# Two chunks of the second MLP's weights converted during the first routing, and the first expert's weight split placed after the token gathers

## The chip, the core and the metric

One NeuronCore of a Trainium2 chip runs the whole program. The metric is the device time of one execution in microseconds (us). The engines are TensorE (PE in the rows, its weight loads PEld), VectorE (DVE), ScalarE (ACT), GpSimd (POOL) and SyncE (SP, which here issues nearly all DMAs). Each engine works through its own instructions in the order in which the program lists them; semaphores make it wait for the others.

## The reference

Three layers follow each other, all in float32 at the interfaces: a decayed linear attention over 8 sequences of 576 tokens, a mixture of 8 experts in which every expert takes exactly 576 of the 4608 tokens by a greedy global order of the gate's logits, and a two-layer MLP with a squared ReLU.

```python
# attention (8 batches, 8 heads, 576 tokens, 64 wide); gamma by head
ret = scale * (q @ k.T) * Dmat          # Dmat = gamma ** (i - j) for i >= j
x = (ret @ v) -> (4608, 512)
# experts: tokens in descending order of logits, each expert takes 576
logits = x @ w_gate
for idx in argsort(-logits.flatten()):  # assign token to expert while it has room
    ...
out[mask_e] = relu(x[mask_e] @ w1[e]) @ w2[e]
# second MLP, 4608 tokens, 512 -> 2048 -> 512
h = relu(x @ w_in); return (h * h) @ w_out
```

`w_in` and `w_out` come as float64 (they are a float32 array times a NumPy scalar), so the kernel has to bring 64-bit numbers to 32 bits itself.

## The kernel before

**Stages.** The program has three stages. Attention (`attention`, up to about 175 us of the span) walks over 36 tiles of 128 tokens; tile t does the key transposes of tile t+2 (L145, L147), the scores of tile t+1 (L167, L171), the part of the state (L199), the values (L207, L210) and the state's update (L181, L187). The result x^T stays in nine SBUF buffers named `big`. The second stage is what is called here the routing gap (about 175 to 219 us): `Router.phase(0)` searches by counting for the 576 tokens of the first expert, on VectorE and TensorE in turns (L401 to L438), while `turn_back` transposes x^T back and writes the rows of x to memory (`xd`, L661 to L665). The third stage alternates `moe(k)` for expert k and one or two calls of `mlp(j)` for 384 tokens each; it takes the rest, with a matmul nearly always on TensorE. There the router's steps for later experts are strewn between the matmuls (`slot`).

**Precision.** Every float32 operand of a large matmul is split into a rounded high part and a low part, and three products are summed (`PAIRS`). So each chunk of weights is split before use: two copies on ScalarE (L631), one subtraction on GpSimd (L632), one on VectorE (L633). `pump()` does this for one chunk and issues the load of a later one; `pump(True)` issues the load alone.

**The second MLP's weights.** `convert` is a generator with 32 units (16 chunks in two halves). One call of `next(filler)` at the end of each attention tile moves all live units one step: load the raw 64-bit half (L559), two steps later three ScalarE operations (L564 to L566), one step later three VectorE operations (L570 to L572), two steps later the write of the 32-bit result to memory (`wd`, L575). Nine chunks (`RES`) are later read back and stay in SBUF: `stay` loads eight of them from `wd` during the first expert, `part` splits them (L690, L691), and the ninth goes through two buffers named `xg`.

**Between routing and the first expert.** The main loop (L892 to L896) takes one step of the router, one or two tiles of `turn_back`, and one `pump`, which splits only once the last one-hot comparison of list 0 is issued (`near`). When the list is there (L513 to L518), `load_tokens` gathers the tokens' rows by five indirect DMAs on GpSimd's queue (L711), `turn` transposes each gathered tile (L719) and splits it into XH (ScalarE, L727) and XL (VectorE, L728). Until three tiles are turned, nothing of the first expert starts; 36 transposes into a scratch tile (L900) keep TensorE busy while the gathers run. Then `moe(0)` begins with L805 (first layer), L810 and L811 (ReLU and its low part), L788 (second layer).

**What sets the order.** There is no scheduler: every engine's order is the order of the Python code. All tiles come from pools with a fixed number of buffers that are handed out in rotation, so a new tile of a name waits until the last reader of the tile some places back is done: `h` has 3 buffers, `ot` 3, `mm` (PSUM) 3, `raw` 3, `big` 9, `xg` 4, and `gs`, the gate's staging tile, 1.

## Time and profile before

| | us |
|---|---|
| median of 3 runs | 1510.81 |
| lowest and highest of them | 1508.19, 1512.13 |
| the profiled execution, as timed | 1512.18 |
| its span in the profile | 1510.4 |
| attention, to the router's first step | 0 to 175.4 |
| routing gap, to the first expert's first matmul | 175.4 to 219.3 |
| experts and second MLP | 219.3 to the end |

The profile is one execution taken by the hardware profiler. Its time lies 1.37 us above the median of the three runs, and 1.78 us of it lie outside the span. All times of instructions are counted from the span's start. A row of the timeline says when an engine did what, and in square brackets how long the engine had stood idle before it and what released it; a row of windows gives the busy time of each engine in a stretch. Matmuls overlap, so a "busy" TensorE says that it had work, not that it was at its peak.

### The profile page before, as it was taken

To read this page: it belongs to the slowest core of one execution; us is meant where nothing else is said; L and a number is where in the kernel's file an instruction comes from. 1 tells how busy PE (TensorE), PEld (TensorE's weight loads), DVE (VectorE), ACT (ScalarE), POOL (GpSimd) and SP (SyncE) were. 2 spreads that over 40 slices of the span, in tenths; PEclk is the share of its full clock that TensorE was granted. 3 is DMA by queue.
4 is the path that set the end of the run, shared out by engine and by line. 5 is a ranking of instruction groups with operands and counts; after the bars stand their busy time and mean duration, and the time that the engine had idled before them with its cause. 6 is when DMAs were issued, how large, how long until landed. Compare 5 with 4: busy or idle time off the path is not lost.

```text
span 1510.4 us, 27450 instructions
## 1 busy us (share of the span) xinstructions
PE 1461.7 (97%) x10599; PEld 1325.1 (88%) x10599; DVE 933.6 (62%) x1965; ACT 688.6 (46%) x1349; POOL 468.6 (31%) x410
## 2 busy tenths in 40 slices
PE   7998879999999999999999999999999999999997
PEld 6777768888988889989988899899888999999896
DVE  4989768767664667656665676566656544454341
ACT  6766544444533345335433354345334454454332
POOL 4555124444311334124213143143112441251110
PEclk9999989999999999999999999999999999999999
DMA  9999477224511326225312153245113352262200
GB/s 335 346 354 359 177 252 265 85 84 125 169 43 63 102 66 194 70 91 160 113 56 95 56 154 119 77 125 162 57 49 102 116 184 64 63 195 77 70 29 21
DMA packets 64354, 201.14 MB, mean 133 GB/s; under 512 B 8416, under 2 KB 8800, under 8 KB 64224
## 3 DMA queue, kind: packets, MB, share of 16 engines
q1 hardware_dynamic: 58272, 179.99, 36.3%
q0 software_dynamic: 5952, 19.40, 3.8%
q8 instruction: 83, 1.36, 0.4%
q14 instruction: 47, 0.39, 0.1%
HBM read 172.10 MB, written 27.26 MB: 132 GB/s over the span
## 4 chain that ended last, share of the span: by engine, by line
PE 84%; DVE 7%; issue 4%; ACT 3%; DMA 1%; POOL 0%; SPq 0%; POOLq 0%; DVEq 0%; ACTq 0%
PE mm L868 25%; PE acc L852 24%; PE acc L788 13%; PE mm L805 13%; PE px L207 2%; PE sc L167 1%; PE mm L719 1%; PE rps L511 1%; DVE cb L572 1%; DVE G L401 1%; DVE A L171 1%; DVE w L633 1%; PE px L199 1%; ACT cb L564 1%; PE pr L145 1%
## 5 line engine op out<-in xcount | busy, mean ns | idle before, releaser
L632 POOL TENSOR_TENSOR w<-raw,w 128x512 fp32r<-128x512 f32 x212 | 278.4, 1313 | 817.7 <-ACT w L631 783.1
L633 DVE TENSOR_TENSOR w<-raw,w 128x512 fp32r<-128x512 f32 x212 | 226.9, 1070 | 193.5 <-ACT w L631 192.5
L631 ACT ACTIVATE w<-raw 128x512 fp32r<-128x512 f32 x424 | 253.1, 623 | 78.3 <-PE acc L788 62.1
L852 PE MATMUL acc<-big,h 128*128 128x512 f32 x972 | 251.2, 399 | 1.8 <-ACT h L878 1.8
L788 PE MATMUL acc<-h,w 128*128 128x288 f32 x1536 | 223.4, 296 | 0.0
L852 PEld LDWEIGHTS acc<-big,h 128*128 128x128 f32 x972 | 180.8, 189 | 38.6 <-ACT h L878 2.9
L788 PEld LDWEIGHTS acc<-h,w 128*128 128x128 f32 x1536 | 208.5, 188 | 0.7 <-DVE h L811 0.4
L874 ACT ACTIVATE r<-mm 128x384 f32<-128x384 f32 x192 | 93.8, 488 | 237.7 <-PE mm L868 217.8
L878 ACT ACTIVATE h<-r 128x384 fp32r<-128x384 f32 x192 | 100.8, 525 | 216.7 <-DVE r L876 216.7
L852 PE MATMUL acc<-w,h 128*128 128x512 f32 x756 | 196.0, 398 | 2.9 <-DVE h L845 2.9
L876 DVE TENSOR_TENSOR r<-mm,r 128x384 f32<-128x384 f32 x192 | 106.0, 552 | 128.6 <-ACT r L874 127.9
L868 PE MATMUL mm<-YH,big 128*128 128x384 f32 x864 | 171.6, 340 | 0.0
L852 PEld LDWEIGHTS acc<-w,h 128*128 128x128 f32 x756 | 140.1, 189 | 29.9 <-DVE h L845 3.8
L805 PE MATMUL mm<-XH,w 128*128 128x288 f32 x1024 | 160.5, 299 | 0.8 <-ACT XH L727 0.7
L868 PEld LDWEIGHTS mm<-YH,big 128*128 128x128 f32 x864 | 151.2, 189 | 7.5 <-ACT YH L794 0.8
L845 DVE TENSOR_TENSOR h<-r,h 128x384 fp32r<-128x384 f32 x192 | 110.9, 578 | 65.6 <-ACT h L878 65.6
L805 PEld LDWEIGHTS mm<-XH,w 128*128 128x128 f32 x1024 | 143.2, 189 | 1.8 <-ACT XH L727 0.9
L868 PE MATMUL mm<-YH,w 128*128 128x384 f32 x672 | 134.0, 341 | 0.0
L868 PEld LDWEIGHTS mm<-YH,w 128*128 128x128 f32 x672 | 118.2, 189 | 4.3
L810 ACT ACTIVATE h<-mm 128x288 fp32r<-128x288 f32 x128 | 52.5, 410 | 103.2 <-PE mm L805 97.8
L868 PE MATMUL mm<-YL,big 128*128 128x384 f32 x432 | 92.8, 337 | 0.0
L805 PE MATMUL mm<-XL,w 128*128 128x288 f32 x512 | 89.1, 296 | 0.0
(171 smaller groups left out, 1749.8 us busy)
## 6 DMA issues: line engine op xcount, KB each, us to landing
raw<-we SPq DMA_DIRECT2D x128, 512.0 KB, 3.6
raw<-wd SPq DMA_DIRECT2D x84, 512.0 KB, 3.3
qk<-att SPq DMA_DIRECT2D x36, 512.0 KB, 6.7
craw<-wm SPq DMA_DIRECT2D x32, 512.0 KB, 6.7
v<-att SPq DMA_DIRECT2D x36, 256.0 KB, 5.4
wd<-cb SPq DMA_DIRECT2D x32, 256.0 KB, 5.6
xd<-YH SPq DMA_DIRECT2D x18, 256.0 KB, 3.7
xd<-YL SPq DMA_DIRECT2D x18, 256.0 KB, 3.7
```

The costliest lines, as they stand in the source:

```text
L631: nc.scalar.activation(w[:, 0], c, AF.Copy)
L632: nc.gpsimd.tensor_sub(w1[:, 1], raw[:, :512], w1[:, 0].bitcast(F32))
L633: nc.vector.tensor_sub(w2[:, 1], raw[:, 512:], w2[:, 0].bitcast(F32))
L788: nc.tensor.matmul(acc[part][d][:, :288], w2[:, wi, d * 128:(d + 1) * 128], h[:, xi, :288], start=(f == 0 and i == 0), stop=(f == 7 and i ...
L805: nc.tensor.matmul(p[:, :288], w1[:, wi, g * 128:(g + 1) * 128], X[xi][:, g, 288 * part:288 * part + 288], start=(g == 0 and i == 0), stop ...
L810: nc.scalar.activation(h[:, 0, :288], p[:, :288], AF.Relu)
L845: nc.vector.tensor_sub(h[:, 1], s, h[:, 0].bitcast(F32))
L852: nc.tensor.matmul(acc[t], h[:, xi, t * 128:(t + 1) * 128], w2[:, wi], start=(f == 0 and i == 0), stop=(f == 15 and i == 2))
L868: nc.tensor.matmul(p[:, :384], w1[:, wi, g * 128:(g + 1) * 128], Y[xi][:, g, o:o + 384], start=(g == 0 and i == 0), stop=(g == 3 and i == 2))
L874: nc.scalar.activation(r, p[:, :384], AF.Relu)
L876: nc.vector.tensor_mul(s, p[:, :384], r)
L878: nc.scalar.activation(h[:, 0], s, AF.Copy)
```

## The change

The change has five parts. (1) `convert` leaves out chunks 13 and 15 (`LATE`), so it has 28 units; one extra `next(filler)` ahead of the tile loop starts it one tile earlier. Conversions on ScalarE now stand behind tiles 1 to 28 instead of 2 to 33, on VectorE behind tiles 2 to 29 instead of 3 to 34. (2) `late_load` reads the raw 1 MB of each of the two chunks into a `big` buffer that x^T has left, after 12 and after 22 turned tiles; `late_units` converts them in place, with `ot` and `h` tiles as scratch: ScalarE's six operations of chunk 13 when `near` is set, VectorE's six behind the first four gathers, then ScalarE's six of chunk 15, and VectorE's six of chunk 15 behind the three turned tiles. (3) In the main loop nothing is split any more; the first split stands behind the first four gathers, the second behind the three turned tiles. So `moe(0)` begins with two chunks split instead of three. (4) The scratch transposes become 30, and 6 after each of the three turned tiles. (5) The last gates of the attention are issued inside the last tile, with two `gs` buffers; `stay` and `part` lose the two chunks, and `part` takes a step in every round of the second half of `moe(0)` instead of in every other one, the two late chunks first.

```diff
@@ gate, attention
-            gs = wk.tile([128, 512], F32, name="gs", bufs=1)
+            gs = wk.tile([128, 512], F32, name="gs", bufs=2)
...
         decay(1)
+        next(filler)
         for t in range(NT):
...
+            if t == NT - 1:
+                next(ready)
+                last = gate(32, 35)
+                next(last)
             values(t)
             if t % 9 != 8:
                 state(t)
             if t == NT - 2:
                 ready = rt.prep(0, 32)
-            if t >= NT - 2:
                 next(ready)
+            if t == NT - 1:
+                next(last)
...
-        last = [gate(32, 35), gate(35, 36, "sp")]
-        for g in last:
-            next(g)
-        for g in last:
-            next(g)
+        for _ in gate(35, 36, "sp"):
+            pass
@@ convert
+LATE = (13, 15)
+def scaled(nc, raw, b, n):
+    nc.scalar.activation(b, raw[:, :, 1].bitcast(F32), AF.Copy, scale=2.0 ** -112)
+    nc.scalar.activation(n, raw.bitcast(U16)[:, :, 1], AF.Copy, scale=2.0 ** -13, bias=2.0 ** 23)
+    nc.scalar.activation(n.bitcast(I32), n, AF.Copy, bias=-2.0 ** 23)
+def narrowed(nc, b, n, s, dst):
+    u = b.bitcast(I32)
+    nc.vector.tensor_scalar(s, u, -2147483648, None, op0=OP.bitwise_and)
+    nc.vector.scalar_tensor_tensor(s, u, 3, s, op0=OP.logical_shift_left, op1=OP.bitwise_or)
+    nc.vector.tensor_tensor(dst.bitcast(I32), s, n.bitcast(I32), op=OP.add)
...
-    todo = [(f, h) for f in range(16) for h in range(2)]
+    todo = [(f, h) for f in range(16) if f not in LATE for h in range(2)]
@@ body
+        def late_load(f):
+            late[f] = w = gp.tile([128, 2048], F32, name="big", bufs=9)
+            nc.sync.dma_start(w.bitcast(I32) if wide else w[:, :1024], a["wm"][f].bitcast(I32) if wide else a["wm"][f])
+        def late_units():
...
+            for f in LATE:
+                raw = late[f].bitcast(I32).rearrange("p (n t) -> p n t", t=2)
+                for h in range(2):
+                    if h:
+                        x = [wk.tile([128, 2, 384], R, name="h", bufs=3).bitcast(F32)
+                             .rearrange("p a b -> p (a b)")[:, :512] for _ in range(3)]
+                    else:
+                        x = [wk.tile([128, 512], F32, name="ot", bufs=3) for _ in range(3)]
+                    scaled(nc, raw[:, 512 * h:512 * h + 512], x[0], x[1])
+                    work.append((x, late[f][:, 512 * h:512 * h + 512]))
+                yield
+                for x, dst in work:
+                    narrowed(nc, x[0], x[1], x[2].bitcast(I32), dst)
+                work = []
+                yield
...
-            for n in ((0, 1), (2, 3), (4, 5), (6,), (7,)):
+            for n in ((0, 1), (2, 3), (4, 5)):
...
-                        if part and f % 2:
+                        if part:
                             next(parter, None)
...
-            pump(0 not in near)
+                turns += 1
+                if turns in (12, 22):
+                    late_load(LATE[turns == 22])
+            if 0 in near and 0 not in listed:
+                next(units, None)
+                near.clear()
+            pump(True)
...
-        warm = ps.tile([128, 512], F32, name="mm", bufs=3)
-        for _ in range(36):
-            nc.tensor.transpose(warm[:, :128], idn, idn)
+        for _ in range(4):
+            next(loader)
+        next(units, None)
+        pump()
+        next(units, None)
+        warm(30)
         while state["turned"] < 3:
+            n = state["turned"]
             next(loader)
+            if state["turned"] > n:
+                warm(6)
         pump()
+        next(units, None)
```

VectorE between the first turned tokens and the router's next step, before (XL is the tokens' low part, w a split weight chunk, m the first result of the router's preparation for list 1):

```order
L728 TENSOR_TENSOR XL<-mm,XH 128x4x128
L728 TENSOR_TENSOR XL<-mm,XH 128x4x64
L728 TENSOR_TENSOR XL<-mm,XH 128x4x128
L633 TENSOR_TENSOR w_3324<-raw,w_3324 128x512
L375 TENSOR_REDUCE m<-L 128x36
L376 TENSOR_TENSOR V<-L,m 128x288
```

And now, at the same place:

```order
L769 TENSOR_TENSOR XL<-mm,XH 128x4x128
L646 TENSOR_TENSOR w_3317<-raw,w_3317 128x512
L558 TENSOR_SCALAR ot<-ot 128x512
L559 SCALAR_TENSOR_TENSOR ot<-ot 128x512
L560 ISA big<-ot 128x1024
L558 TENSOR_SCALAR h<-h 128x512
L559 SCALAR_TENSOR_TENSOR h<-h 128x512
L560 ISA big<-h 128x1024
L378 TENSOR_REDUCE m<-L 128x36
```

The six operations that narrow chunk 15 stand ahead of the router's preparation; the six of chunk 13 stand in the same way ahead of the first weight split, behind the list's last operation.

ScalarE between the list's one-hot columns (HC) and the first tokens' high part (XH), before:

```order
L499 ACTIVATE HC<-h_113,rt 128x36x5
L631 ACTIVATE w_3217<-raw 128x512
L631 ACTIVATE w_3218<-raw 128x512
L631 ACTIVATE w_3247<-raw 128x512
L631 ACTIVATE w_3248<-raw 128x512
L727 ACTIVATE XH<-mm 128x4x128
```

And now, from the end of chunk 13's conversion on:

```order
L553 ACTIVATE h<-h 128x512
L644 ACTIVATE w_3221<-raw 128x512
L644 ACTIVATE w_3222<-raw 128x512
L551 ACTIVATE ot<-big 128x512
L552 ACTIVATE ot<-big 128x512
L553 ACTIVATE ot<-ot 128x512
L551 ACTIVATE h<-big 128x512
L552 ACTIVATE h<-big 128x512
L553 ACTIVATE h<-h 128x512
L768 ACTIVATE XH<-mm 128x4x128
```

Chunk 15's six operations stand between the first weight split and XH, and they write the `ot` and `h` tiles that VectorE reads for chunk 13.

GpSimd from the attention's last product on, before (xg are gathered rows):

```order
L154 TENSOR_TENSOR qh<-qk,qc 128x512
L632 TENSOR_TENSOR w_3217<-raw,w_3217 128x512
L632 TENSOR_TENSOR w_3247<-raw,w_3247 128x512
L711 DMA xg<-xd,idx 128x512
L711 DMA xg<-xd,idx 64x512
```

And now:

```order
L154 TENSOR_TENSOR qh<-qk,qc 128x512
L752 DMA xg<-xd,idx 128x512
L752 DMA xg<-xd,idx 64x512
L752 DMA xg<-xd,idx 128x512 x2
L645 TENSOR_TENSOR w_3221<-raw,w_3221 128x512
L752 DMA xg<-xd,idx 128x512
```

Four gathers come ahead of the first split and one behind it.

## Rows read from the trace of the kernel before

**Rows 1.** Page: busy time, share of the span and instructions of each engine.
```profile
PE 1461.7 (97%) x10599; PEld 1325.1 (88%) x10599; DVE 933.6 (62%) x1965; ACT 688.6 (46%) x1349; POOL 468.6 (31%) x410
```
**Rows 2.** Windows: start:end, length, busy us of each engine, granted clock, DMA share, GB/s.
```profile
150.00:155.00 5.00, 4.98 (x60) 4.27 (x62) 3.21 (x6) 0.97 (x3) 1.27 (x1) 0.66 0.68 224
...
200.00:220.00 20.00, 12.43 (x96) 11.03 (x94) 12.22 (x38) 5.75 (x11) 7.82 (x8) 0.74 0.74 243
...
400.00:500.00 100.00, 100.00 (x587) 90.77 (x586) 57.10 (x135) 39.24 (x78) 20.04 (x19) 1.00 0.23 77
```
**Rows 3.** Timeline, tile 3: start, length, engine, line, operation, [idle before <- releaser].
```profile
25.21 0.69 DVE L171 TENSOR_TENSOR A<-sc,mask 128x512 f32<-128x512 f32 x1 [1.24 <-PE sc L167]
```
**Rows 4.** Timeline, the attention's last tiles.
```profile
152.87 1.97 PE L207 MATMUL px<-A,v 128*64 128x128 f32 x16
...
158.82 1.09 PE L207 MATMUL px<-A,v 128*64 128x128 f32 x16
...
160.77 1.09 DVE L570 TENSOR_SCALAR cs<-cb 128x512 int32<-128x512 int32 x1
...
164.15 1.66 PE L167 MATMUL sc<-qk,kT 64*128 64x128 f32 x16
```
**Rows 5.** Timeline, one unit of the conversion on VectorE, and the router's first step.
```profile
170.12 0.42 DVE L570 TENSOR_SCALAR cs<-cb 128x512 int32<-128x512 int32 x1
...
171.39 0.69 DVE L572 CUSTOM_DVE_ANT_0 cb<-cs,cn 128x1024 uint16<-128x1024 uint16 x1
...
172.83 0.28 ACT L132 ACTIVATE gs<-sp 128x128 f32<-128x128 f32 x1 [0.70 <-PE pr L136]
...
175.41 0.95 DVE L401 SCALAR_TENSOR_TENSOR G<-kf,B,rt 128x448 f16<-128x448 f32 x2
```
**Rows 6.** Groups by line: the conversion's first ScalarE operation, count | busy, mean ns.
```profile
L564 ACT ACTIVATE cb<-craw 128x512 f32<-128x512 f32 x32 | 21.4, 668 | 0.0
```
**Rows 7.** Windows of 2 us in the routing gap, with the DMA share and rate last.
```profile
198.00:200.00 2.00, 0.34 (x5) 0.33 (x4) 1.71 (x4) 0.78 (x2) 0.00 (x0) 1.00 1.02 382
...
202.00:204.00 2.00, 0.01 (x1) 0.00 (x0) 1.79 (x10) 0.31 (x1) 0.00 (x0) 0.68 0.50 159
```
**Rows 8.** Timeline from the one-hot columns to the first expert's first matmul.
```profile
203.69 0.49 ACT L499 ACTIVATE HC<-h,rt 128x180 f16<-128x180 f16 x1 [2.67 <-DVE h L497]
...
207.80 1.35 DVE L633 TENSOR_TENSOR w<-raw,w 128x512 fp32r<-128x512 f32 x1 [0.96 <-DMA raw<-we]
...
209.26 1.03 DVE L517 TENSOR_TENSOR idx<-ids 128x4 int32<-128x4 f32 x1
...
210.58 1.13 POOL L711 DMA_INDIRECT xg<-xd,idx  x1 [0.30 <-DVE U L526]
...
217.50 0.85 PEld L719 LDWEIGHTS mm<-idn,xg 64*128 64x128 f32 x8 [2.80 <-DMA xg<-xd,idx]
...
219.27 1.89 PE L805 MATMUL mm<-XH,w 128*128 128x288 f32 x8 [0.69 <-ACT XH L727]
```
**Rows 9.** The line of the gathers, list 0 alone: from issue to landing.
```profile
DMA to landing us min/median/max: 3.5/3.8/4.6
```
**Rows 10.** Timeline, VectorE and TensorE in the first rounds of expert 0.
```profile
220.29 1.36 DVE L633 TENSOR_TENSOR w<-raw,w 128x512 fp32r<-128x512 f32 x1 [0.35 <-ACT w L631]
...
221.58 0.44 DVE L375 TENSOR_REDUCE m<-L 128x36 f32<-128x288 f32 x1
...
226.46 1.78 DVE L633 TENSOR_TENSOR w<-raw,w 128x512 fp32r<-128x512 f32 x1
...
228.30 1.81 DVE L401 SCALAR_TENSOR_TENSOR G<-kf,B,rt 128x448 f16<-128x448 f32 x2
...
229.91 0.49 PE L424 MATMUL rps<-A,G 128*128 128x64 f16 x5 [1.60 <-DVE G L401]
```
**Rows 11.** Timeline, two waits of TensorE in the first call of the second MLP.
```profile
300.50 1.91 PE L852 MATMUL acc<-w,h 128*128 128x512 f32 x7 [1.45 <-DVE h L845]
...
304.20 0.25 PE L483 MATMUL rps<-ones,DT 128*72 128x128 f16 x1 [1.79 <-DVE es L478]
```

32 lines of the change are left out of this document (19 added, 13 removed).

## The prediction

> **What bounds the kernel now.** I read the busy shares first: TensorE has work for 97% of the span [rows 1]. In the windows by stage it is full once the experts run (100 us of 100 between 400 and 500), and far from full in the routing gap, 12.43 us of 20 between 200 and 220 at a granted clock of 0.74 [rows 2]. So whatever this change brings or costs has to come out of the attention's end, the gap and the first rounds of expert 0; behind them it moves only if TensorE is made to wait. I then went through the timeline of those stretches in order of time and asked of every wait who ends it. In the attention TensorE sets the pace, and the conversion on ScalarE and VectorE only adds small stalls. In the gap the router's chain sets it, VectorE and TensorE in turns, up to the token list; then the gathers; then the turned tokens. In the first rounds of expert 0 it is VectorE: TensorE stands 1.60 us at L424 for VectorE's L401 [rows 10]. That last point matters most here.
>
> I count from the profiled execution, 1512.18 us; it lies 1.37 above the median of 1510.81, and the forecast goes to the median. A measurement of this kernel can tell about 0.3% from no change, 4.5 us, so "the same" is 1506.3 to 1515.3.
>
> **The attention.** One conversion unit on VectorE runs from 170.12 to 172.08, 1.96 us [rows 5]. Removed are four units of 32, and the conversion starts one tile earlier, so what is saved lies behind the last five tiles, and a unit is added behind tile 2. There VectorE has 1.24 us of idle [rows 3] for 1.96 of work: at most +0.7, at least 0, since rt.start's long casts that follow may swallow it; I take +0.4. At the end VectorE's L570 at 160.77 (1.09 us instead of 0.42) pushes the masks, and the scores at 164.15 take 1.66 us, held by it [rows 4, 5]; I put 0.5 of that down to the conversion and 0.2 to two short waits of TensorE for ScalarE. The regrouped gates drop the wait for the single `gs` buffer (0.70 at 172.83 [rows 5]), but their first four matmuls now stand ahead of the last tile's values; net -0.2. Together -0.9, between 0 and -2.5: the lower end is for the case that TensorE keeps its clock. Between 150 and 155 it was granted 0.66 [rows 2], and the same 16 matmuls took 1.97 us there against 1.09 later [rows 4]; over that tile about 1.6 us. The idle before that drop comes from a unit that stays (the last one, behind tile 29), so I don't count on it. The router's first step, at 175.41 [rows 5], comes 0.5 earlier.
>
> **The gap up to the list.** The two late loads are 2.1 MB, at the 382 GB/s of a full queue [rows 7] 5.5 us of DMA, and they stand in SP's queue ahead of the later writes of x. The queue is full up to 202 and half empty from there [rows 7], so the last write is through at about 207.5 instead of 202.5. The gathers read those rows, but can't start before the list does. So hidden, with about 1 us to spare; without that cover up to +2. ScalarE's copies wait for a write twelve tiles back; the second load delays this only for the last two tiles, which nobody awaits.
>
> **The list.** VectorE's first split starts at 207.80 and takes 1.35; the list's copy stands behind it, then an index operation takes 1.03 beside GpSimd's split, and the first gather is issued at 210.58 [rows 8]. With both splits behind the gathers the list is copied when its matmuls end, about 207.9, and the gather can go at 208.55: -2.0.
>
> **The turned tokens.** VectorE goes on with chunk 13: two units, 3.9 us, 209.5 to 213.4. ScalarE is done with HC at 204.18 [rows 8]; its six operations of chunk 13 at 0.67 each [rows 6] end at about 208.1. But chunk 15's six take the same scratch tiles and wait until VectorE has read them: the last ends at 214.85, and only then the first XH, which stood at 214.98 before. The gathers are no longer what is waited for: issued at 208.55, 209.85 and 211.1 and 3.8 us in flight [rows 9], the third is there at about 216. The scratch transposes rotate through the three `mm` buffers, so the third tile is turned behind the first XL; I get the third XH at 218.1 and L805 at 218.15 instead of 219.27 [rows 8]: -1.1 of the -2.0.
>
> A rule of the Trainium skill speaks against this part. The rows show gathers landing within 4.6 us while VectorE's index and split operations run [rows 9]. "SBUF — State Buffer", section "SBUF: two separate sides", says that VectorE's two-port operations lock GpSimd out of writing the descriptors of its own DMAs, so that such a DMA seems to be held up by VectorE; chunk 13's six operations now stand exactly beside the gathers. By the row the sum stays; by the page the gathers would be held, which is a rival below.
>
> **VectorE in expert 0.** The second weight split ended at 221.65 (220.29 and 1.36 [rows 10]); 1.0 earlier now. Behind it come chunk 15's two units, 3.9 us, and only then L375, at 224.55 instead of 221.58 [rows 10]: +3.0. What is queued behind: the router's preparation, the first low part L811, XL of the fourth tile, and L401, for which TensorE's L424 waits. From L375 to the end of L401 were 8.53 us, of which some 2.7 were VectorE operations held by GpSimd's splits (L633 1.78, L401 1.81, each about 1 us over its free length) and 0.65 were waits for XH. If none of this comes back, L401 ends at -0.4 against before; if all does, at +3.0. GpSimd still does the same three splits there, but one should meet reduces and PSUM reads, which ran at their free length beside it; and ScalarE is no longer late with XH. So I take off 1.0 and 0.65: +1.3. The -1.1 at L805 does not enter the sum, since L424 is later than all of it.
>
> **Behind that.** TensorE is full. GpSimd gets four more subtractions in expert 0's second half and four fewer in the first MLP call; the two waits there, 1.45 and 1.79 us [rows 11], could go or stay: I take 0, between -3.2 and +1. Two reads and four writes fewer on the queue release nobody.
>
> **Sum.** +0.4 - 0.9 + 1.3 = +0.8 against 1512.18; on the median 1510.81 + 0.8 = 1511.6.
>
> **Rivals.**
> *VectorE becomes the bound outright (slower).* One mechanism: chunk 15's six operations stand ahead of the router's preparation. If the third XH is as late as before and one GpSimd split holds one of the six (1.0), L375 comes at 226.5, +4.9, and if none of the 8.53 us is won back, TensorE stands over 5 us before L424 and comes back at a lower clock, as at 150 to 155; a 12-matmul group then loses 1.3. -0.5 + 4.9 + 1.3 = +5.7: 1516.5. It decides from L424 at about 234.5 on. For it: VectorE has almost no idle between 219 and 230. Against: TensorE's order gives it two groups to do in the meantime.
> *The stalls go (faster).* TensorE keeps its clock at 150 (-1.6), L401 comes at -0.4 instead of +1.3, and the two waits of rows 11 go (-3.2): +0.8 - 1.6 - 1.7 - 3.2 = -5.7: 1505.1. For it: all of these are small and sensitive to order. Against: the idle ahead of 150 has its cause in what stays.
> *The loads in x^T's places are not hidden.* The last write of x lands at 210.9 (207.2 and a landing of 3.7 us) and the gathers start 0.3 later than before instead of 2.0 earlier; everything behind comes as before plus chunk 15: +2.7, 1513.5. The change then doesn't bring the earlier gather that it makes room for.
> *The gathers are held by chunk 13.* If gathers 2 to 4 wait for the six operations to end at 213.4, the third lands at about 219, L805 stands at 220.6, and the sum grows by 2.4: 1514.0. The page named above would have it so; the rows so far don't.
>
> **How the numbers follow.** Forecast 0.50 (its own range 1508.6 to 1514.6), VectorE the bound 0.20, stalls go 0.13, loads not hidden 0.10, gathers held 0.07. Faster by over 0.3%: more than half of the second rival and the low tail, 0.11. Slower: most of the first, and some of the tails, 0.20. The same: 0.69. The range 1506.0 to 1517.0 leaves out the far ends of the first two rivals.
>
> **What would show it.** The first gather's issue should be near 208; the first XH right behind ScalarE's last operation of chunk 15; six VectorE operations ahead of the router's preparation; TensorE's wait at L424's successor longer than 1.60 and ending near 231; the router's first step near 174.9. Wrong would be: gathers landing after 217, a wait at the writes of x, a granted clock below 1 behind 232, or TensorE's waits at 300 and 304 gone.

## Result

The changed kernel takes 1520.97 us (median of six runs, 1519.79 to 1523.00) against 1510.99 for the kernel before (six runs on the same chip, 1508.19 to 1512.13): a ratio of 1.0068 with a 95% interval of 1.0057 to 1.0079. It is slower by 10 us. The forecast was 1511.6, 0.8 above the 1510.81 before, with a range to 1517.0; so the prediction said hardly any change, and the result lies 4 us outside its range. The profiled execution of the changed kernel has a span of 1519.3 us, that of the kernel before 1510.4.

The page's row of busy times, which answers to [rows 1]:

```profile
PE 1466.1 (96%) x10611; PEld 1327.9 (87%) x10611; DVE 934.1 (61%) x1965; ACT 687.6 (45%) x1349; POOL 468.6 (31%) x410
```

TensorE's busy time is 4.4 us longer, for the same matmuls and 12 scratch transposes more, some of them at the lower clock; the other half of the 9 us is waiting. Nearly all of both arises before the second expert begins. The next table is worked out from the timelines: the start of the router's first step on VectorE (`G`, L401 before, L404 after), of the first gather, of the first matmul of expert 0, of the first MLP call and of expert 1, and in the last two columns how long expert 0 and the first MLP call took. The later rows belong to the experiments below. From expert 1 on the distance between any of these kernels and the kernel before stays as it is, within 1 us, to the end, so the column of expert 1 decides.

| kernel | router | gather | expert 0 | MLP 0 | expert 1 | expert 0 takes | MLP 0 takes |
|---|---|---|---|---|---|---|---|
| before | 175.4 | 210.6 | 219.3 | 278.8 | 361.1 | 59.5 | 82.2 |
| after | 177.0 | 213.9 | 224.1 | 289.5 | 369.6 | 65.3 | 80.1 |
| b_loads | 174.1 | 215.1 | 225.0 | 284.7 | 367.1 | 59.7 | 82.3 |
| b_load1 | 174.1 | 212.0 | 221.6 | 281.6 | 362.5 | 60.0 | 80.9 |
| b_loads_late | 174.6 | 209.9 | 223.2 | 283.1 | 365.3 | 59.9 | 82.2 |
| b_split | 175.0 | 208.7 | 216.1 | 275.5 | 360.4 | 59.4 | 84.9 |
| b_split2 | 173.9 | 207.7 | 215.3 | 275.1 | 357.2 | 59.8 | 82.1 |
| b_split2p | 172.3 | 206.1 | 213.7 | 274.7 | 353.3 | 61.0 | 78.6 |
| u_split2 | 174.5 | 213.1 | 223.8 | 286.5 | 363.7 | 62.7 | 77.2 |
| u_skip15 | 174.5 | 213.1 | 222.9 | 283.7 | 363.6 | 60.8 | 79.9 |
| u_yh | 175.6 | 214.0 | 221.9 | 287.0 | 368.4 | 65.1 | 81.4 |
| u_13only | 175.0 | 210.1 | 219.2 | 281.1 | 361.0 | 61.9 | 79.9 |
| u_13split2 | 173.8 | 208.0 | 218.9 | 279.6 | 358.2 | 60.7 | 78.5 |

One caution belongs to it. The attention code of b_loads, b_load1, b_loads_late, b_split, b_split2 and b_split2p is that of the kernel before, and its end, the router's first step, lies between 172.3 and 175.4 from one profiled execution to the other. So a difference of one or two microseconds between two profiles is not an effect by itself; the timed ratios decide, and the columns show where. It helps to count from the router's first step: the gather comes 35.2 us behind it in the kernel before, 33.7 in b_split, 36.9 in the changed kernel, 38.6 in u_skip15 and 41.0 in b_loads.

**The gathers.** The forecast had the first gather at 208.55, 2.0 us sooner than before [rows 8]. It goes out at 213.87. The list is there at 209.7, as the row of VectorE's index operation (L520) shows, but the last six writes of x are only issued from 204.37 on and the fetch of weights behind them at 209.51, where the kernel before had reached it at 202.97. Even ScalarE, which copies x into the staging buffers, waits 3.51 us for an earlier write. Timeline of the changed kernel, from the second late load (L688) to the first matmul of expert 0:

```profile
195.44 1.26 SPq L688 DMA_DIRECT2D big<-wm  x1
...
204.37 4.93 SPq L678 DMA_DIRECT2D xd<-YL  x6
...
204.41 1.25 ACT L677 ACTIVATE YL<-mm 128x512 f32<-128x512 f32 x2 [3.51 <-DMA xd<-YL]
...
209.51 2.16 SPq L655 DMA_DIRECT2D raw<-we  x3
...
209.68 0.16 DVE L520 TENSOR_TENSOR idx<-ids 128x4 int32<-128x4 f32 x1
...
213.87 1.22 POOL L752 DMA_INDIRECT xg<-xd,idx  x1 [47.60 <-DMA raw<-we]
...
217.67 1.12 PE L760 MATMUL mm<-idn,xg 128*128 128x128 f32 x4 [2.74 <-DMA xg<-xd,idx]
...
224.13 1.29 PE L846 MATMUL mm<-XH,w 128*128 128x288 f32 x8
```

The profile names a fetch of weights as what ended GpSimd's idle time, but the gather reads rows that the last writes of x bring, and the fetch stands right behind them in the same queue. The last write whose landing the trace records was issued at 206.95 and landed 5.1 us later, at 212.04, and the very last one was issued at 208.96, after that. In u_13only, where the last write had landed at 208.42, before the list, the gather followed the list's last index operation by 0.9 us; here it follows it by 4.0. The windows of 4 us (last two columns: share of the DMA engines' time and GB/s) show the queue. The kernel before:

```profile
200.00:204.00 4.00, 0.81 (x7) 0.32 (x4) 3.39 (x21) 0.91 (x2) 0.00 (x0) 0.84 0.75 264
204.00:208.00 4.00, 2.87 (x38) 2.71 (x39) 2.93 (x5) 1.34 (x3) 0.68 (x1) 0.50 0.89 335
208.00:212.00 4.00, 4.00 (x21) 4.00 (x20) 3.93 (x12) 1.15 (x2) 3.18 (x3) 0.50 0.54 179
```

The changed kernel:

```profile
200.00:204.00 4.00, 1.76 (x12) 1.10 (x12) 3.27 (x16) 0.90 (x2) 0.00 (x0) 0.94 0.96 334
204.00:208.00 4.00, 1.39 (x21) 1.34 (x22) 3.70 (x10) 3.50 (x7) 0.00 (x0) 0.50 1.05 405
208.00:212.00 4.00, 3.80 (x32) 3.71 (x31) 2.91 (x13) 1.62 (x3) 0.00 (x0) 0.50 1.04 367
```

Over these 12 us it moves 4.4 MB (334, 405 and 367 GB/s for 4 us each) where the kernel before moves 3.1 MB.

**From the gathers to expert 0.** Expert 0 is 4.9 us late, 1.6 more than the first gather. While the gathered tiles are turned, TensorE's clock is at half. Its row of the third turn, and the window of 218 to 222 (granted clock after the five busy times):

```profile
222.22 1.11 PE L760 MATMUL mm<-idn,xg 128*128 128x128 f32 x4
```

```profile
218.00:222.00 4.00, 4.00 (x20) 3.31 (x18) 1.11 (x2) 1.68 (x4) 3.19 (x3) 0.50 0.59 162
```

The same in u_yh below, which has the same TensorE instructions here, a gather as late (214.03), and full clock:

```profile
220.60 0.63 PE L764 MATMUL mm<-idn,xg 128*128 128x128 f32 x4
```

```profile
218.00:222.00 4.00, 3.82 (x31) 3.14 (x31) 1.22 (x3) 2.47 (x6) 3.33 (x4) 1.00 0.65 153
```

From the first turn to expert 0 it is 6.5 us in the changed kernel and 4.0 in u_yh. The six scratch transposes behind each turned tile stand in this chain, 1.25 to 1.54 us each time at half clock and 0.82 to 0.87 at full; no run leaves them out.

**The first rounds of expert 0.** Here the forecast had L375, the start of the router's preparation, at 224.55 and TensorE's wait behind it near 231. VectorE and those who wait for it, in the timeline of the changed kernel (L646 is the split, L558 to L560 are chunk 15's steps, L378 is the old L375, L427 the old L424):

```profile
225.03 1.37 DVE L646 TENSOR_TENSOR w<-raw,w 128x512 fp32r<-128x512 f32 x1 [0.34 <-ACT w L644]
226.32 0.41 DVE L558 TENSOR_SCALAR ot<-ot 128x512 int32<-128x512 int32 x1
...
229.29 0.69 DVE L560 CUSTOM_DVE_ANT_0 big<-h 128x1024 uint16<-128x1024 uint16 x1
229.90 0.45 DVE L378 TENSOR_REDUCE m<-L 128x36 f32<-128x288 f32 x1
...
229.35 0.41 ACT L851 ACTIVATE h<-mm 128x288 fp32r<-128x288 f32 x1 [4.35 <-DVE h L559]
...
232.87 1.12 PE L760 MATMUL mm<-idn,xg 128*128 128x128 f32 x4 [4.90 <-DVE h L852]
233.63 2.27 PE L846 MATMUL mm<-XH,w 128*128 128x288 f32 x8
...
238.70 0.32 PE L427 MATMUL rps<-A,G 128*128 128x64 f16 x5
```

The split, chunk 15's six steps and the router's preparation stand in one row on VectorE, without a gap. The low part of the first hidden tile (L852) is behind them, and TensorE's next transpose takes the PSUM buffer that L852 reads: 4.90 us of standing still, and the eight matmuls after it take 2.27 us in place of the 1.29 that the same row of the code took at 224.13. In [rows 10] the only wait here was 1.60 us. L427 comes 8.8 us later than L424 did.

### The profile page after: what moved, and what is told of

It is laid out like the page before. It is cut to its first block, busy times and chain, and to the rows that moved or that the text cites. A ratio compares the mean times of both kernels' runs of the same rounds, so it can differ in the third digit from the quotient of the medians.

```text
span 1519.3 us, 27459 instructions
## 1 busy us (share of the span) xinstructions
PE 1466.1 (96%) x10611; PEld 1327.9 (87%) x10611; DVE 934.1 (61%) x1965; ACT 687.6 (45%) x1349; POOL 468.6 (31%) x410
## 4 chain that ended last, share of the span: by engine, by line
PE 81%; DVE 8%; issue 5%; ACT 3%; DMA 2%; POOL 0%; SPq 0%; POOLq 0%; DVEq 0%; ACTq 0%
PE mm L909 24%; PE acc L893 23%; PE acc L829 13%; PE mm L846 12%; PE px L207 2%; PE sc L167 2%; DVE w L646 1%; PE mm L760 1%; PE rps L514 1%; DVE cb L560 1%; DVE G L404 1%; DVE A L171 1%; PE px L199 1%; PE pr L145 1%; ACT w L644 1%
## 5 line engine op out<-in xcount | busy, mean ns | idle before, releaser
L646 DVE TENSOR_TENSOR w<-raw,w 128x512 fp32r<-128x512 f32 x212 | 231.3, 1091 | 194.8 <-ACT w L644 194.8
L829 PE MATMUL acc<-h,w 128*128 128x288 f32 x1536 | 223.8, 296 | 0.7 <-DVE h L852 0.5
L886 DVE TENSOR_TENSOR h<-r,h 128x384 fp32r<-128x384 f32 x192 | 110.6, 576 | 65.1 <-ACT h L919 63.3
L851 ACT ACTIVATE h<-mm 128x288 fp32r<-128x288 f32 x128 | 52.6, 411 | 112.8 <-PE mm L846 106.2
```

Source lines behind the costliest of these rows:

```text
L646: nc.vector.tensor_sub(w2[:, 1], raw[:, 512:], w2[:, 0].bitcast(F32))
L829: nc.tensor.matmul(acc[part][d][:, :288], w2[:, wi, d * 128:(d + 1) * 128], h[:, xi, :288], start=(f == 0 and i == 0), stop=(f == 7 and i ...
L851: nc.scalar.activation(h[:, 0, :288], p[:, :288], AF.Relu)
L886: nc.vector.tensor_sub(h[:, 1], s, h[:, 0].bitcast(F32))
```

## Experiments

Names that begin with b_ are edits of the kernel before, names that begin with u_ edits of the changed kernel. Ratios are to the kernel before, timed beside it on the same chip, with 95% intervals; the changed kernel has 1.0068 on this scale.

### The late loads

Theory A was a sum of four places: a stretch at half clock in the attention, the two late loads, chunk 15's steps ahead of the router's turn, and the second half of expert 0. The loads were tried first, as they alone can be put into the kernel before without anything else of the change.

b_loads:
```
                 next(turner, None)
+                turns += 1
+                if turns in (12, 22):
+                    w = gp.tile([128, 2048], F32, name="big", bufs=9)
+                    nc.sync.dma_start(w.bitcast(I32), a["wm"][13 if turns == 12 else 15].bitcast(I32))
```

> The kernel before with two loads of 1 MB each from the second MLP's wide weights at the 12th and the 22nd turn, into places of x^T that are free by then; nothing reads them. They have the places and the size of the change's loads, and nothing else of the change is there. Theory A: the last writes of x go out later, the first gather with them by 2 to 4 us (212.6 to 214.6), and the end by as much, 1513 to 1515. Rival, the prediction's own: the loads end beside work that is longer, the gather stays at 210.6 and the end at 1511.

1.0044 (1.0028 to 1.0061), 6.6 us. The first gather goes out at 215.09, 4.5 us late, and expert 0 and all behind it come 5.7 to 6.0 us late. Expected was 2 to 4, so theory A has the place, and too small a price. The timeline of this kernel shows two things that the price was worked out without. ScalarE's copies (L664) wait for the staging buffers `YH` and `YL`: the loads push the writes, the writes hold the copies, and the last writes are issued late. And the fetch of weights (L642), which the first splits wait for (L631, 8.18 us), stands behind those writes; in this kernel the list's copy and its index (L517) still stand behind a split on VectorE, as in [rows 8].

```profile
195.14 0.60 ACT L664 ACTIVATE YH<-mm 128x512 f32<-128x512 f32 x1 [0.99 <-DMA xd<-YH]
...
200.46 1.22 ACT L664 ACTIVATE YL<-mm 128x512 f32<-128x512 f32 x2 [2.39 <-DMA xd<-YL]
...
206.60 7.52 SPq L642 DMA_DIRECT2D raw<-we  x4
...
211.08 2.40 ACT L631 ACTIVATE w<-raw 128x512 fp32r<-128x512 f32 x4 [8.18 <-DMA raw<-we]
...
213.78 1.03 DVE L517 TENSOR_TENSOR idx<-ids 128x4 int32<-128x4 f32 x1
...
215.09 1.13 POOL L711 DMA_INDIRECT xg<-xd,idx  x1 [0.30 <-DVE U L526]
```

b_load1 is the same edit with one load.
```
-                if turns in (12, 22):
+                if turns == 12:
```

> The kernel before with one load of 1 MB, at the 12th turn, in place of two. Theory A (from the router's first step to the first expert the moved bytes set the time, so each load costs what it takes at the full queue's 380 to 400 GB/s, 2.7 us): the gather and the first expert come 2.5 to 3.5 us later, the end 1514 to 1515. Rival (the queue has idle time for one load, and the second was the one too many): 1511 to 1512.

1.0026 (1.0015 to 1.0038), 3.9 us. The rival, that one load fits into idle time of the queue, falls. The second load costs 2.7 us more, by the two ratios.

b_loads_late issues both loads behind the first four gathers.
```
         assert next(turner, None) is None
         ...
+        for _ in range(4):
+            next(loader)
+        for f in (13, 15):
+            w = gp.tile([128, 2048], F32, name="big", bufs=9)
+            nc.sync.dma_start(w.bitcast(I32), a["wm"][f].bitcast(I32))
         while state["turned"] < 3:
```

> The kernel before with the two loads of 1 MB again, now issued behind the first four gathers in place of between the writes of x. If what costs is that 2 MB stand ahead of the last writes of x in one full queue: the gather is at 210.6 as before, and the end within 1 us of 1511. If the bytes cost wherever they are moved in this stretch, by holding up the weights and the gathers: 1513 to 1517.

1.0029 (1.0017 to 1.0042), 4.4 us. The first gather is back at 209.92, but now the gathered rows and the weights stand beside 2 MB of loads: the second turned tile begins at 218.22, where the kernel before began its at 217.50, and expert 0 starts 4.0 us late. The one gather whose landing is recorded, issued at 212.58, landed 8.8 us later; in the kernel before none took over 4.6 [rows 9]. So it is not only that the loads stand ahead of the last writes of x: in either of the two places tried the bytes cost.

### The split behind the gathers

b_split takes this one part of the change to the kernel before.
```
-            pump(0 not in near)
+            pump(True)
         assert next(turner, None) is None
+        for _ in range(4):
+            next(loader)
+        pump()
         warm = ps.tile([128, 512], F32, name="mm", bufs=3)
```

> The kernel before with only the split of the first weight block moved behind the four gathers (and before the warming transposes). Theory A: the first gather goes out 2 us sooner, as the prediction had it (208.6 in place of 210.6), and the end comes 1 to 2 us sooner, 1509 to 1510. Rival: the router's turn on VectorE, which comes behind the split, is what sets the end, and the split now stands in its way: 1511 to 1513.

1.0001 (0.9991 to 1.0010). The first gather goes out at 208.65, as the prediction had it (208.55), and the first MLP call begins 3.3 us sooner than before. Then 2.6 of the 3.3 are lost inside that call: it takes 84.9 us in place of 82.2. The time is the rival's, but not for its reason: expert 0, where the split was to stand in the way of the router, takes 59.4 us in place of 59.5. The cause is in the order of the code. The kernel before makes two splits in the gap and one behind the turned tokens; with the move only one of the first two is left. In expert 0 VectorE makes 17 in both, so the missing one is made in the first MLP call, 8 there in place of 7, and TensorE waits longer for the low parts behind them. Waits of TensorE in the first MLP call (who waited, for whom, us in total, times, longest), in b_split:

```profile
PE acc L852 <- DVE h L845: 5.1, 4, 1.6
```

and in b_split2, which makes two splits behind the gathers:

```profile
PE acc L852 <- DVE h L845: 2.9, 2, 1.5
```

```
         for _ in range(4):
             next(loader)
         pump()
+        pump()
```

> The kernel before with the split of the first weight block moved behind the four gathers, and two splits there in place of one, so that as many are made ahead of the first expert as before. With one only, the first MLP began 3.3 us sooner and lost 2.5 again, with two weight splits more in it than before and TensorE waiting three times in place of once for VectorE behind them. Theory A (the missing split is what gave the time back): the first MLP begins 2.5 to 3.5 sooner and the second expert too, 1507.5 to 1508.5. Rival (what is won at the gathers is taken by something else in the first MLP, the router of the second expert or the fetches): 1510.5 to 1511.5. Second rival (the second split stands on VectorE ahead of the router's turn): the first MLP begins less than 2 us sooner, 1509 to 1510.

0.9982 (0.9972 to 0.9993), 2.7 us faster than the kernel before, with the first MLP call back at 82.1 us. The expectation speaks of two splits more in that call of b_split; there is one. The profile alone, 3.9 us sooner at expert 1, overstates it by the earlier end of its attention.

The changed kernel makes one split too few as well: 1 before expert 0 against 2, and 8 in the first MLP call against 7. u_split2 adds the same `pump()` there.
```
         next(units, None)
         pump()
+        pump()
         next(units, None)
         warm(30)
```

> The changed kernel with two weight splits behind the gathers in place of one. Theory A (as in the kernel before, the split that was not made ahead comes back in the first MLP as waits for VectorE): 2 to 3 us sooner, 1518 to 1519. Rival (VectorE is full ahead of the router's turn in the changed kernel, so a second split there delays the turn by its 0.7 to 1.4 us, and the eight steps on the resident chunks have shortened the first MLP already): 1520.5 to 1522.

1.0027 (1.0014 to 1.0041): 0.41% less than the changed kernel's 1.0068, some 6 us, twice what was expected. Expert 0 takes 62.7 us in place of 65.3 and the first MLP call 77.2 in place of 80.1. Two of TensorE's waits in these stages show both halves. In expert 0, where the changed kernel stood 4.90 us:

```profile
PE mm L760 <- DVE h L852: 2.6, 1, 2.6
```

And in the first MLP call, the changed kernel and then u_split2:

```profile
PE acc L893 <- DVE h L886: 3.6, 3, 1.6
```

```profile
PE acc L893 <- DVE h L886: 1.5, 1, 1.5
```

The rival, that VectorE has no room for a second split ahead of the router's turn, falls for this kernel: the split goes into time in which the late gathers are waited for. In u_13split2 below, whose gathers are early, it doesn't.

### Chunk 15

u_13only sends only chunk 13 through the gap.
```
-LATE = (13, 15)
+LATE = (13,)
...
-                if turns in (12, 22):
-                    late_load(LATE[turns == 22])
+                if turns == 12:
+                    late_load(13)
```

> The changed kernel with chunk 13 alone taken in the gap; chunk 15 goes through memory as before, so one late load, its six VectorE operations ahead of the router's turn and its scratch in the first expert's h tiles are gone. Theory A: the six operations and the scratch cost 4 us and the second load 1 to 2: 1515 to 1517. Rival (chunk 15 is the whole loss, the rest was hidden as predicted): 1511 to 1512. Second rival (the loss is in attention and in the first load, chunk 15 costs under 1 us): 1520 or more.

1.0006 (0.9995 to 1.0016): no difference from the kernel before, and all of the change's loss gone, more than theory A gave. It is the rival's number, and half its reason. Chunk 15's load (2.7) and its steps (5.4, next) account for 8.1 of the 9.4 us between the two kernels; but the rest is not hidden, as the rival has it. This kernel still has one load (3.9 us by b_load1), the missing split (2.9) and the early step (2.0), and against them stand the earlier gathers (2.7 by b_split2) and the eight steps on the resident chunks (3.3, below). These make 2.8 where 0.9 (-0.8 to 2.4) was timed, so they agree only within the intervals of the terms.

u_skip15 keeps both loads and leaves out chunk 15's conversion; chunk 13's weights stand in for its own, so the results are of other numbers.
```
             for f in LATE:
+                if f == 15:
+                    return
...
-                    w = late[f][:, cut] if c < 0 else raw9[c][:, cut] if c < 6 else last[h]
+                    w = late[13][:, cut] if c < 0 else raw9[c][:, cut] if c < 6 else last[h]
```

> The changed kernel with both late loads, but without chunk 15's own conversion: its three pairs of steps on ScalarE and its six on VectorE are left out, and the place of chunk 15's weights is filled from chunk 13's, so the results of the second MLP are of other numbers. Theory A (the loads cost by themselves what they cost in the kernel before, 6 us, and chunk 15's steps and scratch some 3 more): the first gather stays at 213.9, the first step of the first expert comes at 224 or a little sooner, the router's turn is 3 us or more sooner, and the end 2 to 4 us sooner than the changed kernel's, 1517 to 1519. Rival (with the gather as late as it is, chunk 15's steps stand beside waits and cost nothing): 1521. Second rival (chunk 15's steps are nearly all of the loss): 1512 to 1514.

1.0032 (1.0016 to 1.0049), 0.36% or 5.4 us less than the changed kernel. The gather is as late as before the edit but for the attention's end (213.09), and expert 0 takes 60.8 us in place of 65.3. TensorE's wait for the router in that stage is then of the size of [rows 10]:

```profile
PE rps L427 <- DVE G L404: 1.2, 2, 1.0
```

So the steps of chunk 15 cost 4.5 us in expert 0, of which 3.7 are their own length on VectorE (226.32 to 229.98 in the changed kernel).

u_yh asks whether it is the steps or their scratch: in the changed kernel the first `h` of expert 0 (L851) waits 4.35 us for a step of chunk 15, whose scratch lies in the `h` tiles.
```
             for f in LATE:
+                if f == 15:
+                    y = wk.tile([128, 6, 512], F32, name="YH", bufs=1)
...
-                    if h:
+                    if f == 15:
+                        x = [y[:, 3 * h + i] for i in range(3)]
+                    elif h:
```

> The changed kernel with chunk 15's scratch in the buffer from which x was written (free once the last x write is through) in place of the h tiles of the first expert and the output tiles. Its six steps on VectorE stay where they are, ahead of the router's turn. Theory A (the steps themselves, 3.7 us on VectorE ahead of the router's turn, are the cost; the h tiles only show it): the first expert takes 64 to 65 us as in the changed kernel and the end stays at 1520 to 1521. Rival (the first expert's h waits 4.4 us for the scratch, and TensorE 4.9 us behind it): TensorE's third turn comes 3 us or more sooner and the end 2 to 4 us sooner, 1517 to 1519.

1.0053 (1.0035 to 1.0072), which overlaps the changed kernel's interval. Expert 0 takes 65.1 us, and TensorE stands as long as before, with no `h` tile in the way any more:

```profile
PE mm L764 <- DVE h L856: 4.9, 1, 4.9
```

The scratch isn't what makes expert 0 long. Chunk 15's steps are, by their place in VectorE's order. Expert 0 begins 2.2 us sooner here; that is TensorE's full clock while the tiles are turned, shown above, and whether the scratch has a part in that is not shown.

### The attention

u_early removes the one early step of the converter from the changed kernel.
```
         decay(1)
-        next(filler)
         for t in range(NT):
```

> The changed kernel without the one early step of the converter ahead of the first tile of attention. Theory A (the loss is a sum of four places: a stretch at half clock at 36 to 43 us, the two late loads in the x writes' way, chunk 15 ahead of the router's turn, the second half of the first expert): the granted clock at 36 to 43 us is 1.00 again, the router's first step on VectorE comes 1.6 us or more sooner (175.4 or less), and the end 1 to 2 us sooner, 1519 to 1520. Theory B (the first gather waits for the last write of x, which waits for the loads, so what attention gives back is lost again): the router's step is as early, but the first gather stays within 0.5 us of 213.9 and the end within 0.5 us of 1521.

1.0043 (1.0029 to 1.0056), 0.25% less, 3.8 us; that is more than was expected. The router starts at 173.7, the first gather is at 211.14. In the changed kernel's profile the router's tables (L364 to L367), a converter step and the masks follow each other on VectorE from 30 to 36 us; TensorE waits 2.16 us for the masks, until 36.39, and its clock is at half from there. Windows of 8 us (after the engines' busy times: granted clock, DMA share, GB/s), the changed kernel:

```profile
36.00:44.00 8.00, 7.61 (x76) 6.67 (x78) 5.26 (x10) 4.60 (x11) 2.22 (x2) 0.57 0.59 178
```

u_13only and u_skip15, whose code is the same up to there:

```profile
36.00:44.00 8.00, 7.29 (x116) 6.04 (x118) 7.66 (x14) 6.68 (x16) 2.39 (x3) 1.00 0.80 255
```

```profile
36.00:44.00 8.00, 7.64 (x130) 6.40 (x132) 7.66 (x14) 6.28 (x16) 2.89 (x3) 1.00 0.89 275
```

In these two there was no half clock, though TensorE had idled as much before it (busy 5.48, 5.43 and 5.39 us of the 8 from 28 to 36), and their router started at 175.0 and 174.5. So this stretch is something that an execution of this code can have, not something that it must have. u_rt4 moves the router's tables one tile on.
```
-            if t == 3:
+            if t == 4:
                 rt.start(rf)
```

> The changed kernel with its early converter step, but the router's tables (the clears and the conversions of VectorE that fell together with a converter step in the fourth tile) one tile later. Theory A (the meeting of the two on VectorE made TensorE wait 2.2 us, and the clock fell behind that): the granted clock at 36 to 43 us is 1.00 and the end is 2 to 3 us sooner, 1518 to 1519, as without the early step. Rival (the meeting only moves to the next tile, which has no gap either): the half clock comes about 4 to 5 us later, and the end stays at 1521.

1.0061 (1.0038 to 1.0083), not told apart from the changed kernel, though its clock at 36 to 43 us was full. The interval holds the changed kernel's 1.0068 and u_early's 1.0043, so theory A's explanation of u_early, the meeting with the tables, is neither shown nor excluded by it. b_early has the early step alone in the kernel before.
```
         decay(1)
+        next(filler)
         for t in range(NT):
```

> The kernel before with the one early converter step ahead of the first tile of attention and nothing else of the change. Theory A (the early step alone costs what the changed kernel won without it): 2 to 3 us, 1513 to 1514.5. Rival (it costs only where the clock falls behind it by chance, and otherwise nothing): within 1 us of 1511.4, with the router's first step between 174 and 175.5.

1.0013 (1.0001 to 1.0025), 2.0 us, between the two theories. So the early step costs something by itself, 0.2 to 3.8 us, and by u_early it may cost more in the changed kernel; why is not settled.

b_split2g adds the change's edits at the end of the attention, without the early step, to b_split2.
```
-            gs = wk.tile([128, 512], F32, name="gs", bufs=1)
+            gs = wk.tile([128, 512], F32, name="gs", bufs=2)
...
+            if t == NT - 1:
+                next(ready)
+                last = gate(32, 35)
+                next(last)
             values(t)
```

> The kernel before with the split behind the gathers and two splits there, and the change's edits at the end of attention (gate sums inside the last tile, two buffers for them), without the early converter step. Theory A (the router starts 0.5 us or more sooner, and with it the writes of x, which the gathers wait for): 0.5 to 1.5 us sooner than with the splits alone, 1507 to 1508. Rival (the writes of x are bound by the moved bytes from the first one on, and start no sooner): 1508.5 as with the splits alone.

0.9988 (0.9976 to 1.0000) against 0.9982 without these edits: nothing gained.

### What is left of the idea, and a faster kernel

b_split2p takes one more part of the change: the halves of the resident chunks in every round of expert 0's second part, 8 for 4.
```
-                        if part and f % 2:
+                        if part:
```

> The kernel before with the split behind the gathers and two splits there, and with the resident chunks' halves taken in every round of the first expert's second part in place of every other (8 for 4), as in the changed kernel. Theory A (in the changed kernel this cost 1 us in the first expert and gave back 2.4 in the first MLP): the first MLP begins about 1 us later than without it and the second expert 1 us sooner, 1507 to 1508. Rival (what the first MLP gave back there came from the late loads' lateness, not from this): 1508.5 to 1509.5.

0.9960 (0.9946 to 0.9975), median 1505.54 us: 6 us faster than the kernel before, and the fastest of all that ran. The first MLP call takes 78.6 us in place of 82.1; it has ten of the resident chunks' subtractions on GpSimd in place of fourteen. Expert 0 takes 61.0 in place of 59.8. Theory A has the places and the 1 us in expert 0, and too small a gain behind it.

u_13split2 is u_13only without the early step and with two splits behind the gathers; it has the eight steps too.
```
         decay(1)
-        next(filler)
...
         pump()
+        pump()
         warm(30)
```

> The changed kernel with chunk 13 alone through the gap, no early converter step, and two splits behind the gathers. Theory A (its one load costs 2.7 us of the full queue and the conversion of chunk 13 lies beside waits, so it stands 2.5 to 3.5 us behind the kernel before with two splits and eight steps, which was at 1505.5): 1508 to 1509. Rival (with one chunk the detour through memory that is saved pays for the load): 1505.5 or less.

0.9988 (0.9976 to 1.0000). What it has more than b_split2p is chunk 13's way through the gap, the gate edits, which gave nothing, and the scratch transposes in other portions. It stands 0.28% or 4.2 us behind it. The time is in theory A's range (1508 to 1509), but not by its mechanism, so that is luck: the load doesn't hold the gather here, which comes 34.2 us behind the router's first step and 33.9 in b_split2p. The time goes between the gather and expert 0, 10.9 us in place of 7.6. Chunk 13's steps don't lie beside waits there: the two splits stand behind them on VectorE and take 3.97 us, partly beside GpSimd's two (213.16 to 215.65), the low part of the turned tokens (L768) stands behind the splits, and TensorE waits for it before the third turn:

```profile
212.23 3.97 DVE L645 TENSOR_TENSOR w<-raw,w 128x512 fp32r<-128x512 f32 x2
...
216.86 1.11 PE L759 MATMUL mm<-idn,xg 128*128 128x128 f32 x4 [2.64 <-DVE XL L768]
```

So the detour through memory that is saved brings nothing that these runs show, and chunk 13's steps, which in the changed kernel lie beside the wait for the late gathers (211.05 to 214.91), stand in the way when the gathers are early. That is read from this one trace; no run takes the load or the steps out of u_13split2 alone.

## Why the prediction was wrong

It had nearly every place in which something happened. It priced two of them far too low, the late loads and VectorE in expert 0, and it missed one, the number of splits made ahead. Of its four signs of being wrong three came: a gather landing after 217 (the third, at 220.4), a wait at the writes of x (3.51 us), and a clock below 1 behind 232 (0.54 from 234 to 238).

**The late loads (taken as hidden; 6.6 us).** This is the largest term and the step that failed most clearly. The working let the last write of x come 5 us later, at 207.5, and held the gathers free because the list would not be there before 208. Two things were wrong in it. It started from 202.5, which is when the kernel before has issued its last writes (the first row below: six from 196.86 to 202.77), not when they are in memory: the last one landed at 204.5, 2.1 us after its issue. So of the 6 us of cover between 202.5 and the first gather at 208.55 two were not there. And in the changed kernel a write itself took longer. The last figure of a row is the median time from issue to landing, for the kernel before (second row) and the changed kernel (third and fourth):

```profile
196.86 5.91 SPq L665 DMA_DIRECT2D xd<-YL  x6
```

```profile
xd<-YL SPq DMA_DIRECT2D x18, 256.0 KB, 3.7
...
xd<-YH SPq DMA_DIRECT2D x18, 256.0 KB, 7.3
xd<-YL SPq DMA_DIRECT2D x18, 256.0 KB, 5.1
```

The forecast had the last write through at 207.5; one that is not yet the last landed at 212.04.

And a full queue is not the only thing that holds the writes: ScalarE's copies wait for staging buffers, so a queue that is behind delays its own next writes. The prediction named this second wait and dismissed it, as it touched only "the last two tiles, which nobody awaits". The gathers await all of them. The rival "the loads are not hidden" had the mechanism, with 0.10 and a gather 0.3 us later than before; measured are 3.3 in the changed kernel and 4.5 in b_loads (1.7 and 5.8 counted from the router's first step). The 6.6 us were measured in the order of the kernel before, where the list stands behind a split; no run takes both loads out of the changed kernel. There the gather comes 3.2 us later than in b_split, counted in the same way, and 4.9 in u_skip15. The window from which the room was read, half empty at 202 to 204 [rows 7], was 2 us long; over 176 to 200 the share was 0.94, and a stretch so full has no room for 5.5 us of bytes.

**The list (-2.0; right, but for what it moved).** Alone, the split behind the gathers brings the first gather to 208.65. The prediction speaks of "both splits behind the gathers"; the code has one there. That expert 0 begins with one split fewer is said in the section on the change, and the prediction put it at nothing without a reason. It came back as 2.6 us in the first MLP call in b_split and some 6 us in the changed kernel (u_split2). No term of the sum, and no rival, had it.

**VectorE in expert 0 (+1.3; 5.8 longer in the profile).** The place was right: chunk 15's six steps stand ahead of the router's preparation, at 3.7 us (3.9 forecast). Even the end of the router's next step (`G`, L404) came as forecast, 13.2 us behind the start of expert 0 (13.3 forecast, from 218.15 to 231.4), though partly by luck: counted so, L378 comes 0.6 sooner than forecast, and of the 1.65 taken off behind it only 1.1 was won. The step that failed is the path. The sum ran by L424, for which TensorE would wait; L427 shows no wait at all. The wait is at the transpose of the fifth gathered tile, 4.90 us, for the low part L852, which stands behind the whole row, and the matmuls behind it run at half clock. The rival "VectorE becomes the bound" had a wait of about 5 us and a lower clock behind it, though at L424, and gave 1516.5, too little by the loads and the missing split.

**The turned tokens (-1.1; +4.9).** The gather is 3.3 us late, and with the half clock while the tiles are turned expert 0 begins another 1.6 behind it. The prediction had no term for this clock, though it priced the one at 150.

**The attention (-0.9; no gain shown).** The early step was put at +0.4; alone it is +2.0 (0.2 to 3.8). The router's first step, forecast 0.5 us sooner, came 1.6 later in the profile. The gains at the end of the attention don't show in b_split2g. A drop of the clock at 150 as in [rows 2] came and went between executions of the same attention code, as the prediction allowed for.

**Behind that (0; -3.3).** Here the prediction was too low on gain: the eight steps of GpSimd in expert 0 shorten the first MLP call, and b_split2p against b_split2 puts it at 0.22%. The bound of -3.2 had the right size, and 0 was chosen; but the bound is by luck, as it stood for the two waits of [rows 11], and waits of TensorE for the same two operations are still there in the changed kernel (3.6 and 1.8 us).

**The gathers held by chunk 13 (rival, 0.07).** They weren't. In u_13split2 four gathers are issued from 207.99 to 213.13 beside chunk 13's steps (208.26 to 212.31). Three landings are recorded, at 3.4 to 3.7 us, not later than the 3.5 to 4.6 of [rows 9]:

```profile
L751 POOL DMA_INDIRECT xg<-xd,idx x4: 908/1032/1255, 208.0 to 212.0; - x4
...
DMA to landing us min/median/max: 3.4/3.5/3.7
```

In u_13only the only recorded landing is 3.3, of the third gather; its first one was there later, 5.0 us after issue, when TensorE's wait for it ended. By the rule of the Trainium skill that stood against it ("SBUF — State Buffer", section "SBUF: two separate sides") they would have been held by VectorE's two-port operations; whether the six steps are such operations no run here shows, and they didn't hold the gathers.

The terms together, from the timed ratios: 6.6 for the two loads, 2.9 for the missing split (b_split against b_split2), 5.4 for chunk 15's steps, 2.0 for the early step, -2.7 for the split behind the gathers and -3.3 for the eight steps make 10.9, and 10.3 were measured (0.68% of 1511). Each has an interval of 1.5 us or more to both sides, and most were measured in the order of the kernel before, so this agrees, and no more. In the changed kernel the missing split was worth 6, not 2.9; it meets chunk 15's steps there, and TensorE's one wait of 4.90 us shrinks for either (2.6 in u_split2). How the overlap divides was not tried. Three things stay open: why the early step costs what it does; whether it costs more in the changed kernel (3.8) than alone (2.0), which the intervals don't tell apart; and what the scratch transposes behind each turned tile cost, which no run changes alone.

## What to carry to other kernels

Before a transfer is called hidden, ask how full its queue is over the whole stretch in which its bytes must pass, and what is last in that queue that somebody awaits; a half-empty window behind the stretch is no room, as the bytes that would fill it are awaited there. When a step that prepares work ahead is moved, count how many such steps are left ahead of the stage that uses them: one too few shows a stage later, as small waits that look like something else. And work that is moved off an engine with slack, onto one that a short stage waits for, costs its full length there.

## What the runs showed of the hardware

A weight split on VectorE (128 x 512) took 0.69 us at 215.24 and 1.37 at 225.03, in the changed kernel; GpSimd's subtraction for a chunk of weights ran beside the second (224.56 to 225.85), and only the issue of a gather beside the first. One megabyte of loads cost 3.9 us (2.3 to 5.7) of the kernel's time in a stretch in which the queue moved 350 GB/s, against the 3.0 us that 1.05 MB take at this rate; the interval holds both. The attention code of the kernel before ended up to 3 us apart in different executions, and the granted clock from 150 to 155 us was 0.66 in three of them (the kernel before, b_loads, b_split) and 1.00 in four (b_load1, b_loads_late, b_split2, b_split2p). The same four transposes of a gathered tile (128 x 128 each) took 1.11 us at half clock and 0.63 at full.
